# A two-layer SSM and GeGLU kernel: partial sums read in PSUM and added to, block 1's kv by four sums, norms in ScalarE, and additions by transfer

## The chip, the cores and the metric

The kernel runs on one core of a Trainium2 chip. The metric is the time of one execution in microseconds on the device. The profile is one execution seen by the hardware profiler. TensorE (PE in the profile, with its weight loads as PEld), VectorE (DVE), ScalarE (ACT) and GpSimd (POOL) have a program each, run in order, and wait for one another by semaphores; transfers are issued by SyncE's queue (SP) and by POOL.

## What is computed

Two layers, each a long convolution with gating (A) and a gated feed-forward network (B), over 2048 tokens of 576 values:

```python
def _A_ref(q, k, v, shift_k, ssm_k, ssm_D):
    ...
    for t in range(ks):
        k_shift = k_shift + k_pad[:, t:t + S, :] * shift_k[:, ks - 1 - t][None, None, :]
    kv = k_shift * v
    ...
    y_f = kv_f * kf_f[None, :, :, :]
    ...
    y = y + kv * ssm_D[None, None, :]
    return q * y
def _B_ref(x, w_gate, w_up, w_down):
    return (_gelu(x @ w_gate) * (x @ w_up)) @ w_down
x = A_q
x = x + _A_ref(_layernorm(x, axis=-1), A_k, A_v, A_shift_k, A_ssm_k, A_ssm_D)
x = x + _B_ref(_layernorm(x, axis=-1), B_w_gate, B_w_up, B_w_down)
x = x + _A_ref(_layernorm(x, axis=-1), A_k, A_v, A_shift_k, A_ssm_k, A_ssm_D)
x = x + _B_ref(_layernorm(x, axis=-1), B_w_gate, B_w_up, B_w_down)
```

Here kv_f and kf_f are Fourier transforms over time of kv and of ssm_k, padded to twice the length, and y is the transform back, cut to 2048. The convolution's result y does not depend on x, so it is computed once and serves both layers.

## The kernel before

**Feed-forward.** The tokens stand in four chunks of 512. A unit is one layer of one chunk, eight in all, numbered in the order (layer 0, chunk 0), (0, 1), (1, 0), (1, 1), (0, 2), (0, 3), (1, 2), (1, 3). They run in passes [0], [1, 2], [3, 4], [5, 6], [7]; a pass goes three times (a third of the 4608 hidden columns each) over its units. One such visit is twelve tiles of gate/up (L1516: 18 matmuls of 512 columns on half the array's rows each, for gate and up side by side), and for each of four rows of tokens a down projection of 24 matmuls of 288 columns (L1535). ScalarE applies the gelu (L1520), VectorE multiplies (hT, L1521), which frees the tile's PSUM buffer; the pool has three. Unit 0's first visit runs with 256 columns at a time (L1441).

**Between units.** x is gated with y (`gate2_steps`, L1165 and L1172 on VectorE), its mean and variance go through ScalarE (L1137) and POOL (L1129, L1144, L1145), VectorE writes the normalised rows xn (`norm` in `prep`, L1194, and a copy of the first 64 columns behind it, L1196), and `spread` has SP transpose them into xnT by two transfers for each of four rows (L1224). SP's queue also carries the weights, which `weights` holds back while rows are about to come. Unit 0 has its own functions, not touched.

**Convolution.** It is done in four blocks of 512 tokens by short transforms of 512 frequencies, as matmuls of the twiddle matrices W with [128, 288] halves of the data, products in the frequency domain, sums over pairs of blocks, and inverse transforms (`inverse`, L340) into y. Block 0 is done in the startup. For block 1 and for its filter's rest (`h1_rest`, the function's `fwd`), `fwd_eo` makes even and odd sums in the two banks of a PSUM tile with four matmuls (L223), ScalarE copies them to a tile eo (L226), and VectorE's `cross` takes sum and difference (L287). For blocks 2 and 3 and their filters, `quarter` makes four sums of one matmul pair each (L261), ScalarE copies each (L263), and VectorE combines them: `both(0, 2)` and `both(1, 3)` (L238 and L239, sum and difference in place), then `even` (L244) and `odd` (L252). Most of these PSUM tiles come from the pool cps, which has one buffer; eo has four.

**Products and sums.** `prod` multiplies a transformed block K with a transformed filter H, real parts first (part 0: L298 and L302), then imaginary (part 1: two products L301 with H's halves exchanged, and L302). In `step(1)` two blocks are summed for each of four frequency tiles kt: `add` (L550) writes the f32 sum zs, `cross` there calls `Conv.both` (L316) and `shift` calls `shifted` (L321), which joins the result with the block before.

**The order.** A planner writes all engines' programs out while it builds the kernel. It keeps model clocks for TensorE, VectorE and ScalarE (`Pace`, with costs C_... for each operation). After each gate/up tile and each pair of down matmuls `fill` lets queues go on: V and U (convolution work on VectorE; U goes first), vq (gating and norms), aq (ScalarE's sums and squares, one for each call), L and spills (POOL's transfers), and Pq (convolution pieces on TensorE, `run_p`). Pieces of Pq go out in order, in the down projection, and among gate/up tiles where `now` says so: before block 1's y is done (`hurry`, after 60 us of the model or while `fresh` pieces are left), for the last pieces of a quarter (`LATE`), or for a y that vq waits for. In the down projection, `run_p(True)` may take the next piece once per row with a buffer of the pool pr instead of cps. `at_start` says at which visit the sums of a chunk's x (`es`) and its gating and norms (`prep`) are entered.

The lines that the planner uses to let a piece go, and the list of visits:

```python
if max(ready(), 0.0 if other else self.ps_free) > t.pe:
    return False
...
at_start = {(0, 0): [("es", 1), ("prep", 1)], (1, 0): [("x", 2)], (2, 1): [("es", 2)],
            (3, 0): [("prep", 4)], (3, 1): [("x", 3)], (4, 1): [("es", 3)], (4, 2): [("prep", 5)]}
```

Of the kernel before, what the change touches and what calls it, by code (L numbers as in the profile page):

```python
# [36 lines left out]
C_SQ, C_TINY = 0.85, 0.6  # L37
N_KC, N_SM, N_EO, N_HR = 4, 4, 4, 3
C_AC, C_AB = 0.76, 0.76
C_TT, C_ST, C_BN, C_NORM, C_HT, C_GELU, C_EVA, C_EVD = 0.76, 0.82, 0.47, 0.62, 0.69, 0.6, 0.66, 0.76  # L40
# [44 lines left out]
class Conv:  # L85
# [9 lines left out]
    def __init__(self, tc, ctx, pace, A_k, A_v, A_shift_k, A_ssm_k, A_ssm_D, ident, psp, cpsp, ypool):  # L95
        self.tc, self.nc, self.t = tc, tc.nc, pace
        self.k2, self.v2, self.hk = A_k[0], A_v[0], A_ssm_k
# [118 lines left out]

    def fwd_eo(self, src, kt, s, h, scale=1.0):
# [11 lines left out]
    def quarter(self, src, out, h, ready, seen, done):  # L229
# [7 lines left out]
        def both(a, b):  # L237
            tt(out=A[b][:], in0=A[a][:], in1=A[b][:], op=add)  # L238
            nc.vector.scalar_tensor_tensor(out=A[a][:], in0=A[a][:], scalar=2.0, in1=A[b][:], op0=ALU.mult, op1=sub)  # L239
            t.on_dve(2 * C_R4)  # L240
# [16 lines left out]
        def one(i):  # L257
            def run():
                ps = self.ps()
                for s in range(2):  # L260
                    nc.tensor.matmul(ps[:, s, 0:HW], lhsT=self.W[:, 2 * i + s, :], rhs=src()[:, i, cols], start=True, stop=True)  # L261
# [3 lines left out]
                self.ps_free = when  # L265
                if i == 2:
                    self.U.append((when + LAG, 2 * C_R4, lambda: both(0, 2)))
                if i == 3:
                    seen(h)
                    self.U.append((when + LAG, 2 * C_R4, lambda: both(1, 3)))  # L270
# [3 lines left out]
        return [(lambda: max(ready(), self.eo_slot()), 0.25, one(i), ("tail", h, i)) for i in range(RT)]  # L274
# [14 lines left out]
    def prod(self, part, K, H, dst=None, own=False):  # L289
# [9 lines left out]
        else:  # L299
            for s in range(2):  # L300
                nc.vector.tensor_tensor(out=pr[:, s, :], in0=K[:, s, :], in1=H[:, 1 - s, :], op=ALU.mult)  # L301
# [17 lines left out]
    def shifted(self, now, prev, part):  # L319

# [91 lines left out]
    def step(self, m, kv=None, loaded=False):  # L412
# [66 lines left out]
        def fwd(kt, s, h):  # L479
            def run():  # L480
                if s == 0 and h == 0:
                    for k in (kt, kt + 2):
                        kc[k] = self.kcp.tile([P, 2, D], BF16, tag="kc", name="kc")
                eo, slot = self.fwd_eo(self.vt_[m], kt, s, h)
                done = t.on_act(C_EVA, t.pe + 0.49 + LAG)
                self.ps_free = done
# [548 lines left out]
def ssm_geglu_kernel(ctx, tc, A_q, A_k, A_v, A_shift_k, A_ssm_k, A_ssm_D, B_x, B_w_gate, B_w_up,  # L1035
# [151 lines left out]
    def prep(ui, j):  # L1187
# [17 lines left out]
        if j >= lag:  # L1205
            tasks.append(norm(j - lag))
# [419 lines left out]
```

## Time and profile before

| | us |
|---|---|
| median of 3 runs (lowest, highest) | 918.87 (918.66, 918.88) |
| profiled execution: time | 918.66 |
| profiled execution: span, first to last instruction | 916.9 |
| first gate/up matmul of unit 0 | 39.1 |
| gate/up matmuls, L1516, 4968 | 541.7 busy |
| down matmuls, L1535, 2304 | 293.3 busy |
| convolution matmuls among gate/up after 39 us | 13 pieces, the last of the first four directly ahead of the down projection |
| y of block 1, four pieces | 131.7 to 142.2 |
| first matmul of unit 1 | 160.2 |

The span leaves out 1.8 us that the time has around it. The granted TensorE clock was 1.00 throughout. A row of the profile names the line, the engine, the operation, what is written and read, the shapes and the count, then busy time, the mean of one in ns, the engine's idle time just before, and what ended it. In the chain of waits in order of time, the columns are start, length and what, in us. TensorE's matmuls overlap, so two of 288 columns that take 286 ns each in their rows take 0.24 us together in the chain.

### The profile page before, as it was taken

The page shows a single profiled execution, that of the slowest core. Times are in us where ns is not written, and L with a number is a line of the kernel's source. Part 1 is how long each engine was busy: PE and PEld are TensorE (multiplying, and loading weights), DVE is VectorE, ACT ScalarE, POOL GpSimd, SP SyncE. Part 2 cuts the span into 40 slices and gives each one's busy share as a digit, 9 for nine tenths or more (in the row PEclk, how much of TensorE's full clock was granted, in tenths as well). Part 3 has the DMA queues.
Part 4 walks back from the last instruction along what each step waited for, and adds up shares of the span by engine and source line. Part 5 has one row for each costly group of instructions (what it writes and reads, how often), then busy time and mean ns, then how long its engine had stood idle before and what let it go on. Part 6 is the DMA issues. An engine that isn't in the chain of part 4 may idle for free.

```text
span 916.9 us, 19346 instructions
## 1 busy us (share of the span) xinstructions
PE 909.1 (99%) x8214; PEld 528.5 (58%) x8214; DVE 608.1 (66%) x1096; ACT 296.6 (32%) x552; POOL 146.1 (16%) x307
## 2 busy tenths in 40 slices
PE   8999999999999999999999999999999999999998
PEld 6786556465565564655655645646546556556555
DVE  7988977578889889798698898652332335432332
ACT  6863225433314134432224123341121224221211
POOL 3433004201114121130013202220000003000000
PEclk9999999999999999999999999999999999999999
DMA  9998978909518706755733912950720721877620
GB/s 257 329 258 254 176 182 161 261 26 258 157 53 196 238 9 123 191 159 145 180 103 96 250 45 60 170 135 11 146 79 1 156 78 22 164 180 173 140 63 26
DMA packets 128666, 130.85 MB, mean 143 GB/s; under 512 B 43586, under 2 KB 120387, under 8 KB 128580
## 3 DMA queue, kind: packets, MB, share of 16 engines
q1 hardware_dynamic: 119232, 93.47, 47.2%
q0 software_dynamic: 9344, 36.14, 11.7%
q8 instruction: 64, 1.05, 0.5%
q14 instruction: 22, 0.18, 0.1%
q10 hardware_dynamic: 4, 0.01, 0.0%
HBM read 108.35 MB, written 11.80 MB: 131 GB/s over the span
## 4 chain that ended last, share of the span: by engine, by line
PE 98%; DVE 1%; ACT 1%; issue 0%; DVEq 0%; ACTq 0%
PE gu L1516 59%; PE dn L1535 31%; PE gu L1441 3%; PE ps L212 1%; PE cps L340 1%; PE cps L261 1%; PE cps L223 1%; PE ps L340 0%; DVE wx L881 0%; PE cps L212 0%; PE cps L818 0%; DVE wx L884 0%; PE ps L223 0%; ACT junk L1137 0%; PE xps L1334 0%; PE ps L895 0%
## 5 line engine op out<-in xcount | busy, mean ns | idle before, releaser
L1516 PE MATMUL gu<-xnT,wgu 64*128 64x512 bf16 x4968 | 541.7, 376 | 0.0
L1516 PEld LDWEIGHTS <-wgu 64*128 64x128 bf16 x4968 | 239.3, 94 | 294.3 <-issue 7.6
L1520 ACT ACTIVATE ga<-gu 128x512 f32<-128x512 f32 x276 | 164.8, 597 | 504.8 <-PE gu L1516 496.4
L1521 DVE TENSOR_TENSOR hT<-ga,gu 128x512 bf16<-128x512 f32 x276 | 189.2, 686 | 194.8 <-ACT ga L1520 192.9
L1535 PE MATMUL dn<-wd,hT 128*128 128x288 bf16 x2304 | 293.3, 286 | 0.0
L1535 PEld LDWEIGHTS <-hT 128*128 128x128 bf16 x2304 | 223.6, 98 | 65.4 <-issue 9.8
L1571 DVE TENSOR_TENSOR x_c<-x_c,dn 128x576 f32<-128x576 f32 x64 | 48.2, 753 | 60.6 <-PE dn L1535 60.2
L1129 POOL TENSOR_SCALAR nm<-s 128x1 f32<-128x1 f32 x60 | 21.1, 352 | 289.2 <-DVE x_c L1566 186.9
L1137 ACT ACTIVATE junk<-x_c,nm 128x576 bf16<-128x576 f32 x48 | 37.0, 772 | 33.7 <-POOL nm L1129 32.2
L1145 POOL TENSOR_TENSOR rstd<-ve,neghalf_t 128x1 f32<-128x1 f32 x62 | 42.2, 681 | 5.2
L470 POOL DMA_DIRECT2D hr<-Hd x32 | 17.5, 547 | 126.3 <-DVE prod L301 119.9
L263 ACT COPY eo<-cps 128x576 f32<-128x576 f32 x32 | 20.4, 639 | 30.7 <-PE cps L261 30.7
L1441 PE MATMUL gu<-xnT,wgu 64*128 64x256 bf16 x432 | 24.6, 269 | 0.0
L1144 POOL TENSOR_SCALAR ve<-ss 128x1 f32<-128x1 f32 x62 | 17.8, 287 | 38.0 <-ACT junk L1137 37.7
L1557 DVE TENSOR_TENSOR ob<-x_c,dn 128x576 bf16<-128x576 f32 x15 | 11.3, 753 | 18.1 <-PE dn L1535 12.9
L302 DVE TENSOR_TENSOR prod<-prod 128x576 bf16<-128x576 bf16 x48 | 22.0, 458 | 1.6
L1441 PEld LDWEIGHTS <-wgu 64*128 64x128 bf16 x432 | 20.8, 94 | 3.4 <-issue 0.9
L355 POOL DMA_DIRECT2D out_dram<-ob x12 | 6.7, 557 | 86.9 <-DVE ob L1557 80.6
L553 DVE TENSOR_TENSOR zs<-zs,prod 128x576 f32<-128x576 f32 x24 | 18.1, 754 | 0.3
L550 DVE TENSOR_TENSOR zs<-sum,prod 128x576 f32<-128x576 bf16 x24 | 18.1, 754 | 0.3
L187 DVE TENSOR_TENSOR kvt<-k,skc 128x1152 bf16<-128x1152 bf16 x24 | 17.6, 753 | 0.2
L1172 DVE SCALAR_TENSOR_TENSOR x_c<-g_t,rstd,x_c 128x576 f32<-128x576 f32 x16 | 13.1, 818 | 6.8 <-POOL rstd L1145 6.6
(158 smaller groups left out, 560.8 us busy)
## 6 DMA issues: line engine op xcount, KB each, us to landing
wgu<-in_B_w_gate_dram SPq DMA_DIRECT2D x45, 576.0 KB, 5.6
wd<-in_B_w_down_dram SPq DMA_DIRECT2D x30, 864.0 KB, 6.6
wgu<-in_B_w_up_dram SPq DMA_DIRECT2D x45, 512.0 KB, 7.7
hr<-Hd POOLq DMA_DIRECT2D x32, 288.0 KB, 5.1
kr<-Kd POOLq DMA_DIRECT2D x24, 288.0 KB, 4.3
Kd<-kc POOLq DMA_DIRECT2D x12, 288.0 KB, 4.1
k<-in_A_k_dram POOLq DMA_DIRECT2D x3, 1008.0 KB, 7.5
wgu<-in_B_w_up_dram SPq DMA_DIRECT2D x45, 64.0 KB, 7.4
```

Source lines behind the costliest of these rows:

```text
L263: nc.scalar.copy(out=A[i][:], in_=ps[:, :, 0:HW])
L302: nc.vector.tensor_tensor(out=dst, in0=pr[:, 0, :], in1=pr[:, 1, :], op=ALU.subtract if part == 0 else ALU.add)
L550: nc.vector.tensor_tensor(out=f[:], in0=self.halves(pr0[:]), in1=self.halves(pr[:]), op=ALU.add)
L1129: nc.gpsimd.tensor_scalar(out=v["nm"][:], in0=v["s"][:], scalar1=-1.0 / D, scalar2=None, op0=ALU.mult)
L1137: nc.scalar.activation(out=junk[:], in_=get_x(), func=ACT.Square, bias=v["nm"][:, 0:1], accum_out=v["ss"][:])
L1145: nc.gpsimd.tensor_tensor(out=v["rstd"][:], in0=ve[:], in1=neghalf_t[:, 0:1], op=ALU.pow)
L1441: nc.tensor.matmul(pair[:, s, e * 256:(e + 1) * 256], lhsT=w[r0:r0 + HK, k, gi * P:(gi + 1) * P], rhs=xnT[r0:r0 + HK, blk_of[k], tok], sta ...
L1516: nc.tensor.matmul(pair[:, s, :], lhsT=w[r0:r0 + HK, k, gi * P:(gi + 1) * P], rhs=xnT[r0:r0 + HK, b, :], start=(k == 0), stop=(k == NKC - 1))
L1520: nc.scalar.activation(out=ga[:], in_=pair[:, 0, :], func=ACT.Gelu_apprx_tanh)
L1521: nc.vector.tensor_tensor(out=hT[:, fi, :], in0=ga[:], in1=pair[:, 1, :], op=ALU.mult)
L1535: nc.tensor.matmul(part[h][:, h, 0:HW], lhsT=hT[:, fi, at * P:(at + 1) * P], rhs=wd[2 * wb + fi // WT][:, fi % WT, h * HW:(h + 1) * HW], s ...
L1571: nc.vector.tensor_tensor(out=xh, in0=xh, in1=acc[:, :, 0:HW], op=ALU.add)
```

## The change

- `quarter`: the four sums are taken in the order 0, 2, 1, 3; the second of each pair is added in PSUM to the first, after ScalarE has copied the first. So ScalarE's second copy is already the sum, and VectorE only makes the difference as twice the first minus the sum (`apart`). Two pieces share a PSUM tile, are marked "pair" and are not taken by `run_p(True)`; `ps_free` is set 0.25 us later.
- Block 1's kv goes through `quarter` as well, in place of eight `fwd_eo` pieces.
- `h1_rest`: its four `fwd_eo` pieces become an even and an odd piece for each of two s (`fwd_sum`): the even sum over both halves is copied to a spare tile (the tile g_t of the gating), the odd one is added to it in PSUM and copied, and VectorE's `differ` makes the other result from the spare tile and PSUM.
- `prod`, part 1: one product that reads H's halves in reverse order, in place of two.
- Block 1's sums for kt 0 and 2: `begin_sum` has POOL copy the first product into the f32 sum by a transfer, `end_sum` adds the second by an adding transfer. `shifted` for kt 0, part 1 is an adding transfer too. The products are put in a new order, with those of kt 3 and 1 between the sums and `cross`.
- Norms of units 1 to 7 become two activations in ScalarE's queue aq, with a bias that POOL multiplies out; vq holds the gating alone.
- `es` and `prep` of chunk 1 are entered at unit 0's third visit.

```diff
     def shifted(self, now, prev, part, transfer=False):
+        if transfer and part == 1:
+            self.nc.gpsimd.dma_start(out=prev[:], in_=now[:], accum_op=ALU.add)
+            return
...
+    def fwd_sum(self, ps, src, kt, s, e):
+        for i in (e, e + 2):
+            for h in range(2):
+                self.nc.tensor.matmul(ps[:, h, 0:HW], lhsT=self.fwd_w(kt, s, i), rhs=src[:, i, h * HW:(h + 1) * HW],
+                                      start=(i == 0), stop=True, skip_group_check=True)
+    def differ(self, dst, eo, ps):
+        self.nc.vector.scalar_tensor_tensor(out=self.halves(dst), in0=self.halves(eo[:]), scalar=2.0, in1=ps[:, :, 0:HW],
+                                            op0=ALU.mult, op1=ALU.subtract)
...
-        def both(a, b):
-            tt(out=A[b][:], in0=A[a][:], in1=A[b][:], op=add)
+        def apart(a, b):
             nc.vector.scalar_tensor_tensor(out=A[a][:], in0=A[a][:], scalar=2.0, in1=A[b][:], op0=ALU.mult, op1=sub)
-            t.on_dve(2 * C_R4)
+            t.on_dve(C_R4)
...
-        def one(i):
+        def one(n, i):
             def run():
-                ps = self.ps()
+                if n % 2 == 0:
+                    A["ps"] = self.ps()
+                ps = A["ps"]
                 for s in range(2):
-                    nc.tensor.matmul(ps[:, s, 0:HW], lhsT=self.W[:, 2 * i + s, :], rhs=src()[:, i, cols], start=True, stop=True)
+                    nc.tensor.matmul(ps[:, s, 0:HW], lhsT=self.W[:, 2 * i + s, :], rhs=src()[:, i, cols], start=(n % 2 == 0), stop=True,
+                                     skip_group_check=True)
...
-                self.ps_free = when
+                self.ps_free = when + LAG
...
-            for s in range(2):
-                nc.vector.tensor_tensor(out=pr[:, s, :], in0=K[:, s, :], in1=H[:, 1 - s, :], op=ALU.mult)
+            nc.vector.tensor_tensor(out=pr[:], in0=K[:], in1=H[:, ::-1, :], op=ALU.mult)
...
+                nc.gpsimd.dma_start(out=f[:], in_=self.halves(pr[:]))
+                return lambda when: self.pr_free.__setitem__(slot, t.pe + 7.0)
...
+                    nc.gpsimd.dma_start(out=sums[(kt, part)][:], in_=self.halves(pr[:]), accum_op=ALU.add)
+                    at[("zs", kt, part)] = t.pe + 6.0
...
+            for kt, part in ((2, 0), (2, 1), (0, 0), (0, 1)):
+                product(kt, 0, part)
+            for kt, part in both:
+                V(0.0, begin_sum(kt, part), eo_done)
+            for kt, part in both:
+                product(kt, 1, part)
+                V(0.0, end_sum(kt, part))
+            for kt, part in ((3, 0), (3, 1), (1, 0), (1, 1)):
+                product(kt, 0, part)
+            for part in range(2):
+                V(2 * C_AB, cross(0, part), get(("zs", 0, part), ("zs", 2, part)))
+                V(2 * C_TB, shift(0, part))
...
+        if other and len(self.Pq[0]) > 4:
+            return False
...
+            self.rest += [(lambda: own.get("free", 0.0), 0.49, even(s), None, "pair"), (lambda: 0.0, 0.49, odd(s), None, "pair")]
...
+            for lo, hi, c0 in ((0, D, 0), (D, XW, 0)):
+                nc.scalar.activation(out=xn[:, lo:hi], in_=x_c[c][:, j, c0:c0 + hi - lo], func=ACT.Identity,
+                                     scale=v["rstd"][:, 0:1], bias=v["nb"][:, 0:1])
...
-        at_start = {(0, 0): [("es", 1), ("prep", 1)], (1, 0): [("x", 2)], (2, 1): [("es", 2)],
+        at_start = {(0, 2): [("es", 1), ("prep", 1)], (1, 0): [("x", 2)], (2, 1): [("es", 2)],
```

167 lines of the change are left out of this document (83 added, 84 removed).

## Prediction

> **What bounds the kernel now.** I read the page's engine table first, then the chain of waits as a table and in order of time.
>
> ```profile
> PE 909.1 (99%) x8214; PEld 528.5 (58%) x8214; DVE 608.1 (66%) x1096; ACT 296.6 (32%) x552; POOL 146.1 (16%) x307
> PE 98%; DVE 1%; ACT 1%; issue 0%; DVEq 0%; ACTq 0%
> ```
>
> TensorE is busy 99% of the span and 98% of the chain. Its 7.8 us without work lie in the startup and after the last matmul, neither of which this change rebuilds. What must be read is whether its time is work or slow matmuls, and that the chain in order of time shows:
>
> ```profile
> 58.40 0.60 PE cps L223 x4
> 58.99 2.07 PE gu L1441 x36
> ...
> 78.51 0.49 PE cps L223 x4
> 79.00 0.49 PE dn L1535 x4
> ...
> 84.64 23.41 PE gu L1516 x216
> 108.05 11.87 PE dn L1535 x96
> ...
> 131.68 1.09 PE cps L340 x8
> ...
> 223.65 0.24 PE cps L261 x2
> ...
> 236.47 0.35 PE cps L261 x2
> ...
> 553.38 0.49 PE cps L340 x4
> ...
> 565.44 0.60 PE cps L340 x4
> ```
>
> Every undisturbed visit costs 23.41 + 11.87 us, and the pieces join without a hole. So the time is the sum of TensorE's pieces, and a convolution piece has two prices: 0.49 us for four matmuls (0.1225 each) between down-projection matmuls (78.51, 553.38), but 0.60 between gate/up matmuls (58.40, 565.44); likewise 0.24 against 0.35 for two. A piece placed among gate/up costs **0.11 us extra**. Freed VectorE, ScalarE or POOL time brings nothing by itself; only fewer matmuls, fewer pieces among gate/up, or a new wait move the end.
>
> **The change, part by part.**
>
> *Block 1's kv by four sums.* Before, eight pieces of four matmuls at L223 (32); after, eight pieces of two at the new `one` (16), as L261 does for blocks 2 and 3. Each piece falls from 0.49 to 0.24-0.25 (or 0.60 to 0.35): 16 x 0.1225 = **-1.96 us**. Four still fall among gate/up from 58 us on, as before, since the same kv half gates them.
>
> *Partial sums in PSUM.* For blocks 2 and 3 and their filters the matmul count stays at eight per half; the second matmul of a pair adds onto what ScalarE has just copied. It must wait for that copy, but the single cps buffer made it wait before too. The planner now books 0.25 us more per step, so steps lie six down matmuls' time apart instead of five; against that one VectorE addition per pair goes:
>
> ```profile
> L238 DVE TENSOR_TENSOR eo<-eo 128x576 f32<-128x576 f32 x16 | 12.0, 751 | 0.0
> L1194 DVE TENSOR_SCALAR xn<-x_c,nm,rstd 128x576 bf16<-128x576 f32 x28 | 16.1, 575 | 1.1 <-POOL rstd L1145 1.1
> L1196 DVE COPY xn<-xn 128x64 bf16<-128x64 bf16 x28 | 5.3, 191 | 1.0
> L550 DVE TENSOR_TENSOR zs<-sum,prod 128x576 f32<-128x576 bf16 x24 | 18.1, 754 | 0.3
> ```
>
> All 16 at L238 go (-12.0 us of VectorE, off the path). Of the 32 L261 pieces three lie among gate/up (at 199.02, 236.47 and 383.68 in the chain). Bounds: none would (-0.33) or two per group of eight, which the LATE rule allows (+0.55). Slower steps and earlier freed eo slots pull opposite ways; I take 0.
>
> *H1's rest* keeps 16 matmuls as two even and two odd pieces. Each even waits until `differ` has freed the spare tile, and a second odd until VectorE has gone through the quarter's queue (0.77 + 1.64 + 1.54 planned). Added up from the planner's costs, the last odd misses the down projection that ends at 84.6: **+0.11** (bounds 0 and +0.44, all four).
>
> *Reversed read in prod.* Two half products become one of 1152:
>
> ```profile
> 27.26 0.76 DVE L298 TENSOR_TENSOR prod<-kc,h 128x1152 bf16<-128x1152 bf16 x1
> 28.43 0.82 DVE L301 TENSOR_TENSOR prod<-kc,h 128x576 bf16<-128x576 bf16 x2
> ```
>
> The pair takes 0.82, the long one 0.76. Of 40 pairs only the startup's last stands on the path (yb, then x_c at 30.40): **-0.07**. The far bound: if the reversed read runs at one element per cycle, the 1152 cost 0.753 (576 in f32) plus 576 / 0.96 GHz as L550 against L302 suggests, about 1.35 us, +0.53 there.
> The Trainium skill (Vector Engine (DVE) Microarchitecture Reference, section 5.1) asks for an innermost step of +-1 and two-byte operands for the double rate, which this read keeps, but lists an operand with a negative step as not measured. By its condition the term is -0.07, by its caveat +0.53; no row here has such a read.
>
> *Norms to ScalarE*: 28 x (575 + 191 ns) leave VectorE; ScalarE gains two activations each (nearest rows L1137 at 772 and the 128x1 warm-up at 203 ns, so 0.98), POOL one small product (L1129 at 352 ns). ScalarE is 32% busy, so 28 us fit; if they pushed a gelu back, TensorE has three gate/up buffers, some 2 x 1.95 - 0.60 - 0.69 = 2.6 us of slack. The deadline is unit 1:
>
> ```profile
> L1224 SPq DMA_TRANSPOSE xnT<-xn x1: 1264/1264/1264, 155.9 to 155.9; - x1
> DMA to landing us min/median/max: 2.5/2.5/2.5
> ```
>
> Unit 1's last transpose lands at 155.91 + 2.5 = 158.4; its first matmul runs at 160.2. Only 1.7 us spare, and TensorE will come 1.9 earlier. Yet the chain shortens too: row 0's norm no longer stands behind row 2's gate, so the four pairs of transposes (2.5 us each on SP's queue) follow the y pieces' 3.1 us spacing instead of piling up until 157.2. I take 0.
>
> *Adding transfers.* Four VectorE additions (754 ns) become four copying and four adding POOL transfers, two shifts (450 ns) two more. Price unseen; nearest rows for 288 KB:
>
> ```profile
> Kd<-kc POOLq DMA_DIRECT2D x12, 288.0 KB, 4.1
> Hd<-h POOLq DMA_DIRECT2D x4, 288.0 KB, 10.3
> ```
>
> Each sum's second transfer waits on POOL for the first; behind it in POOL stand only later sums, loads and spills. Between sum and `cross` lie four products, about one per gate/up tile, 4 x 1.95 = 7.8 us: at 4.1 hidden, at 10.3 not. I take 4.1 to 4.5 (below): 0. Block 1 ends some 4 us earlier, still inside the third visit's gate/up, so its four L340 pieces keep their 0.11 (bounds -0.44 and 0).
> The Trainium skill (DMA: Bandwidth & Descriptors, section "Anatomy of one DMA") fits 2.0 us plus bytes / 436e3; for 295 KB that is an estimate of 2.7 us, below the 4.1 row, and leaves the sum unchanged.
>
> *VectorE relief later.* Some 30 us less before 570 us (12.0 at L238, 16 norms of units 1 to 4 at 0.77, block 1's 4, 40 x 0.06); block 3's last two y pieces, now among gate/up, should make the down projection: **-0.22** (bound +0.22, all four among gate/up).
>
> Sum: -1.96 + 0.11 - 0.07 - 0.22 = **-2.14 us**, 918.66 to 916.5 for the profiled execution. The median is 0.21 above it, so 916.7.
>
> **Rivals.**
>
> 1. *The gain is eaten by misplaced pieces*: -1.96 + 0.11 + 0.22 + 0.55 = -1.1, time **917.8**. For it: every step is booked later. Against: VectorE is freer at each.
> 2. *Slow reversed read*: 0.53 in the startup, and in block 1 eight products at 0.46 + 1.35 against 1.25 booked, 4.5 us that VectorE (21.0 busy of 23.4 at 84.6 to 108) mostly absorbs, perhaps 0.9 lost: -2.07 + 0.53 + 0.9 = -0.6, **918.2**.
> 3. *The sums land late, and it is slower.* At 10.3 us each, first transfers outlast their four products in the down stretch (4.9) by 5.4 and adding ones theirs by 2.5: `cross` stands 7.9 us at VectorE's head, with hT behind it, and TensorE, whose slack is 2.6, loses 5.3: -2.1 + 5.3, **922.0**. It decides once `cross` is over 4.7 us late. For: the startup's Hd spills needed that long, and in this stretch the DMA engines are just as busy (0.94 at 84.6 to 90). Against: the hr load issued there, at 89.1, landed in 4.5 us.
> 4. *Unit 1 comes late, and it is slower.* The early sums and squares of unit 1 now start only at 119.9, one ScalarE task per tile, to 135.5; then eight squares and norms to about 151, landing near 155.6. If block 1's y came four tiles late (7.8), TensorE at 158.2 would wait 5.2: **922.0**.
>
> **How the numbers follow.** About 0.2% (1.84 us) is what a measurement here can tell from no change. Forecast 0.66 (all faster), rivals 1 and 2 0.10 and 0.04 (both within), 3 and 4 0.11 and 0.09 (slower): faster 0.66, same 0.14, slower 0.20. Without a wait the bounds run from -1.96 - 0.33 - 0.44 - 0.22 - 0.07 = -3.0 to rival 2's; that leaves out 0.20, and I stretch the upper end for a small wait: 915.6 to 919.5.
>
> **What would show it.** Right: 16 matmuls of 288 columns fewer; L223's x4 kv pieces as x2 of 0.24 or 0.35; the rest of the chain still gapless with 23.4 + 11.9 per visit; no L238; products of 1152 at 0.75. Wrong: a TensorE gap at about 95-105 with VectorE behind a DMA (rival 3), or before unit 1's first matmul at 158 (rival 4); more than 13 pieces among gate/up (rival 1).

## The result, and the profile after

The changed kernel takes **928.91 us** (median of 4 runs, 928.52 to 929.27) beside 918.76 (918.63 to 918.88) for the kernel before on the same chip: a ratio of 1.011, 95% interval 1.0093 to 1.0128. It is slower by 10 us, where 2 us less had been forecast. The profiled execution has a span of 926.4 us.

The engine table and the first line of the chain of waits, of the changed kernel:

```profile
PE 910.0 (98%) x8198; PEld 528.9 (57%) x8198; DVE 573.2 (62%) x972; ACT 325.8 (35%) x608; POOL 159.8 (17%) x345
PE 90%; DMA 4%; issue 2%; ACT 1%; DVE 1%; POOL 1%; SPq 0%; POOLq 0%; DVEq 0%; ACTq 0%
```

TensorE has the 16 matmuls less that were forecast (8198 for 8214), and VectorE is 35 us less busy. But TensorE holds 90% of the chain instead of 98%: transfers, VectorE, ScalarE and POOL now stand on the path that sets the end. Who made TensorE wait, in the list of waits by engine (total us, times, longest):

```profile
PE gu L1559 <- DVE hT L1564: 6.4, 1, 6.4
PE gu L1559 <- DMA xnT<-xn: 1.5, 2, 0.8
...
PE gu L1559 <- DVE ob L1600: 0.8, 1, 0.8
```

Before, none of these three was on the list. The first is a hole of 6.4 us in unit 0's second visit, which begins at 82 us. VectorE's timeline there (start, length, line, what; in brackets the idle time before it and its releaser):

```profile
96.34 0.76 DVE L315 TENSOR_TENSOR prod<-kc,hr 128x1152 bf16<-128x1152 bf16 x1 [2.42 <-DMA zs<-prod]
...
98.77 0.68 DVE L1564 TENSOR_TENSOR hT<-ga,gu 128x512 bf16<-128x512 f32 x1
104.40 0.76 DVE L313 TENSOR_TENSOR prod<-kr,H 128x1152 bf16<-128x1152 bf16 x1 [4.95 <-DMA zs<-prod]
...
107.47 0.76 DVE L315 TENSOR_TENSOR prod<-kr,H 128x1152 bf16<-128x1152 bf16 x1 [1.81 <-DMA zs<-prod]
...
108.64 0.68 DVE L1564 TENSOR_TENSOR hT<-ga,gu 128x512 bf16<-128x512 f32 x1
```

The next product cannot be written, because the pool of products has three buffers and an adding transfer (zs<-prod) still reads the one whose turn it is. VectorE runs in order, so hT of the next gate/up tile, planned behind the products, stands too: from 98.77 to 108.64 there is none. TensorE fills the PSUM buffers it has and stops. What the transfers took from issue to landing (the list of DMA issues; KB each, median us):

```profile
zs<-sum POOLq DMA_DIRECT2D x4, 288.0 KB, 5.6
zs<-prod POOLq DMA_DIRECT2D x4, 288.0 KB, 12.7
...
Hd<-H POOLq DMA_DIRECT2D x2, 288.0 KB, 12.8
hr<-Hd POOLq DMA_DIRECT2D x1, 288.0 KB, 13.3
```

The copies are zs<-sum, the adding transfers zs<-prod. The last two rows are plain transfers that POOL issued between and right behind the adding ones, and they took as long: what was slow here was every transfer that POOL issued from 91 us on, and no row shows that adding made it longer. From 95 to 98 us, with three to four of them under way, POOL's queue moved 4 of the 611 packets on the DMA engines; the rest were SyncE's.

The hole costs more than its 6.4 us. The stretches around it, with TensorE's busy time and count, its weight loads, VectorE, ScalarE and POOL, then the granted TensorE clock, the DMA engines' busy share and GB/s:

```profile
104.00:106.00 2.00, 0.00 (x0) 0.00 (x0) 1.22 (x2) 0.00 (x0) 0.00 (x0) 0.81 1.07 229
106.00:108.00 2.00, 0.00 (x0) 0.00 (x0) 0.53 (x1) 0.00 (x0) 0.00 (x0) 0.50 1.26 301
...
110.00:112.00 2.00, 2.00 (x12) 0.81 (x10) 1.67 (x3) 0.01 (x1) 0.00 (x0) 0.50 1.12 213
112.00:114.00 2.00, 2.00 (x22) 1.00 (x20) 1.97 (x5) 0.60 (x1) 0.00 (x0) 0.98 1.15 192
```

While TensorE stands, its granted clock falls to 0.50, and it stays there until 112 us: 12 matmuls in 2 us, then 22. The Trainium skill (TensorE: Matmul & The Clock Gate, Part 1, "The HAM clock gate") says that about 3.4 us of idleness bring the array to half rate and that about as long a busy time brings it back. The trace agrees on the half rate, and roughly on the times: the last matmul ends at 102.97 and the clock falls at 105.25, 2.3 us later; matmuls begin again at 109.37 and the clock is back at 112.07, 2.7 us later. In e14 below the two times are 4.3 and 5.6.

**The account.** I measure a visit's excess as its length over what the undisturbed visits take: 23.42 us of gate/up and 11.87 of down projection, with 0.1225 for each convolution matmul in it and 0.11 for each piece among gate/up. Before, the excess of all visits is 0.82; after, 11.70: 8.09 in that visit, 0.89 + 0.89 at unit 1's start (the second wait above), 0.97 in the visit at 816 us (the third), the rest within 0.05 of before. So 916.9 + 10.88 of excess - 1.96 (16 matmuls) + 0.22 (15 convolution pieces among gate/up instead of 13) + 0.34 (first gate/up at 39.40 instead of 39.06) = 926.4, the span.

The second wait is the one that the deadline of unit 1 had threatened. SyncE's transposes for unit 1:

```profile
L1269 SPq DMA_TRANSPOSE xnT<-xn x8: 1222/1265/1707, 154.6 to 166.0; - x8
```

The last lands at 168.54, 10.1 us later than before (158.43). It costs only 1.8 here, because the hole had already made TensorE late.

### The profile page after: what moved, and what is told of

It is laid out like the page before. It is cut to its first block, busy times and chain, and to the rows that moved or that the text cites. A ratio compares the mean times of both kernels' runs of the same rounds, so it can differ in the third digit from the quotient of the medians.

```text
span 926.4 us, 19300 instructions
## 1 busy us (share of the span) xinstructions
PE 910.0 (98%) x8198; PEld 528.9 (57%) x8198; DVE 573.2 (62%) x972; ACT 325.8 (35%) x608; POOL 159.8 (17%) x345
## 4 chain that ended last, share of the span: by engine, by line
PE 90%; DMA 4%; issue 2%; ACT 1%; DVE 1%; POOL 1%; SPq 0%; POOLq 0%; DVEq 0%; ACTq 0%
PE gu L1559 55%; PE dn L1578 28%; PE gu L1484 3%; PE cps L275 1%; DMA Hd<-H 1%; PE ps L213 1%; DMA out_dram<-ob 1%; PE cps L356 1%; DMA zs<-prod 1%; DMA zs<-sum 1%; ACT junk L1188 1%; PE ps L356 0%; DVE wx L931 0%; PE cps L213 0%; PE cps L868 0%
## 5 line engine op out<-in xcount | busy, mean ns | idle before, releaser
L1196 POOL TENSOR_TENSOR rstd<-ve,neghalf_t 128x1 f32<-128x1 f32 x62 | 39.3, 634 | 5.2
L278 ACT COPY eo<-cps 128x576 f32<-128x576 f32 x40 | 25.5, 636 | 33.5 <-PE cps L275 31.0
L1250 ACT ACTIVATE xn<-x_c,nb,rstd 128x576 bf16<-128x576 f32 (+1 forms) x56 | 33.3, 644 | 9.4 <-POOL nb L1200 9.3
L1195 POOL TENSOR_SCALAR ve<-ss 128x1 f32<-128x1 f32 x62 | 21.1, 340 | 45.3 <-ACT junk L1188 44.7
## 6 DMA issues: line engine op xcount, KB each, us to landing
k<-in_A_k_dram POOLq DMA_DIRECT2D x3, 1008.0 KB, 12.2
```

The source lines that it names most:

```text
L278: nc.scalar.copy(out=A[i][:], in_=ps[:, :, 0:HW])
L1195: nc.gpsimd.tensor_scalar(out=ve[:], in0=v["ss"][:], scalar1=1.0 / D, scalar2=EPS, op0=ALU.mult, op1=ALU.add)
L1196: nc.gpsimd.tensor_tensor(out=v["rstd"][:], in0=ve[:], in1=neghalf_t[:, 0:1], op=ALU.pow)
L1250: nc.scalar.activation(out=xn[:, lo:hi], in_=x_c[c][:, j, c0:c0 + hi - lo], func=ACT.Identity, scale=v["rstd"][:, 0:1], bias=v["nb"][:, 0:1])
```

## The experiments

Letters in the expectations stand for the theories named in them. All times are medians beside the kernel before at 918.7 to 918.8 on the same chip; brackets after a ratio are its 95% interval. The milestones are read from each profile: the last of block 1's shifts, unit 1's rows landed, TensorE's waits and the excess as defined above.

### Transfers away, or less in their way

*e1* sums by `add` and shifts on VectorE again; *e2* keeps the transfers and has four product buffers (the pool xn gives two up for the room); *e3* takes only the sums' transfers back:

```diff
e1, e3
-                V(0.0, begin_sum(kt, part), eo_done)
...
-                V(0.0, end_sum(kt, part))
+                V(C_AC, add(kt, 1, part), eo_done)
e1
-                    self.shifted(nyb[(part, kt, sg)], z[(part, kt, sg)], part, kt == 0)
+                    self.shifted(nyb[(part, kt, sg)], z[(part, kt, sg)], part)
e2
-        self.prp = pool("c_pr", 3)
+        self.prp = pool("c_pr", 4)
-    xnp = pool("xn", 4)
+    xnp = pool("xn", 2)
```

> The changed kernel, with block 1's four sums and both shifts made by VectorE additions again, in the changed order of the products. Theory A (the adding transfers land after 7 to 14 us, a product waits until they have read its buffer, and hT waits behind it): the 6.4 us gap of TensorE in the second visit goes, and with it the slower clock there and the late rows of unit 1, which come later only because block 1 did; 916.3 to 917.3 us, 0.2% under the kernel before. Theory B (the norms in ScalarE make unit 1's rows late by themselves): the gap goes, but TensorE still waits some 1.8 us before unit 1; 918.2 to 919.

> The changed kernel with four product buffers in place of three (and two xn buffers in place of four, to make room); the transfers stay. Theory A (the wait is on the product buffer that an adding transfer still reads): the product that finds its buffer taken comes one product, about 2 us, later, so VectorE's waits on the sums' transfers in front of products (10.1 us in the changed kernel) fall by 2 to 6 us, the gap of 6.4 shrinks by as much, and the time falls to 922 to 927. Rival (the wait is for the finished sums, or the DMA engines' load delays the weights): no change from 928.9 beyond 1 us.

> The changed kernel with the four sums made by VectorE again and only the two shifts as adding transfers. Theory A: the shifts are read first by the y pieces some 15 us after they are issued, and land after 6.6 us, so nothing waits: within 0.3 us of the kernel with no transfers, 916.3 to 917.5. Rival (any adding transfer costs, by the load on the DMA engines or on POOL): 1 us or more above the kernel with no transfers.

e1: 927.09 (926.51 to 927.33), ratio 1.009 [1.0075, 1.0105]. The hole is gone (excess of that visit 0.20), so the product buffers did make it. But the time hardly falls: block 1's last shift comes at 134.3 (before: 129.4), unit 1's rows land at 165.35, and TensorE loses 3.52 + 4.73 us there (beyond what before has in these visits, as in all losses below). e2: 928.67 in one run; the hole's 8.09 falls to 3.46, unit 1's loss rises from 1.8 to 6.6. e3: 928.67 (927.46 to 929.24), ratio 1.0103 [1.0086, 1.012]: 1.6 above e1, and all its runs lie above all of e1's, so the rival of its expectation held. The profiles of the two lie 2.7 apart, 1.6 of it at unit 1 and 1.1 in the visit that begins at 425 us; by which way the shifts' transfers, landed at 118, reach there is not shown. So the hole and unit 1's late rows are two costs that **cover each other**: TensorE arrives late at unit 1 by the one, or waits there for the other. That the transfers are the whole loss is refuted.

### Block 1's kv by four sums, alone on the kernel before

*e4*:

```diff
-            if m > 1:
-                self.Pq.extend(self.quarter(lambda: self.vt_[m], out4, h, get(("kv", h)), seen4, done4))
-                continue
-            for kt in range(2):
-                for s in range(2):
-                    self.Pq.append((lambda g=get(("kv", h)): max(g(), self.eo_slot()), 0.49, fwd(kt, s, h)))
+            self.Pq.extend(self.quarter(lambda: self.vt_[m], out4, h, get(("kv", h)), seen4, done4))
```

> The kernel before with one part of the change alone: block 1's kv through quarter (four sums, both as before), with neither the addition in PSUM nor the transfers nor the norms in ScalarE. The count of TensorE's matmuls falls by 16 of 288 columns at 0.1225 us: 1.96 us less, 916.6 to 917.1, if the pieces stay where they were and VectorE's 2 x 1.5 us more additions hide. Rival (VectorE, fuller in the first visits, finishes block 1 later, and unit 1's rows, 1.7 us early before, come late): 917.5 to 919.

934.09 (932.93 to 935.17), ratio 1.0166 [1.0151, 1.0182]: the part that was to bring the gain loses 15 us by itself. VectorE's timeline there:

```profile
85.39 0.69 DVE L1516 TENSOR_TENSOR hT<-ga,gu 128x512 bf16<-128x512 f32 x1 [1.23 <-ACT ga L1515]
...
90.45 1.56 DVE L252 TENSOR_TENSOR kc<-eo 128x288 bf16<-128x288 f32 x4
...
92.52 1.42 DVE L244 TENSOR_TENSOR kc<-eo 128x576 bf16<-128x576 f32 x2
...
94.46 0.75 DVE L298 TENSOR_TENSOR prod<-kc,hr 128x1152 bf16<-128x1152 bf16 x1
```

No part of kc is ready until all four sums are there: the first product with kc begins at 94.5, and VectorE had nothing else to do at 84 to 85 (idle before the hT at 85.39). The last shift comes at 140.0 instead of 129.4, and TensorE waits 12.2 us in three places for transposed rows (8.2 of them before unit 1, the rest at unit 5, near 609 us). Some 7 us of the excess lie around unit 5, and what makes its rows late was not looked into; so not all of the 15 us is block 1.

### What is left without the transfers: kv as before, norms as before

*e5* is e1 with block 1's kv by `fwd_eo` (the lines of e4's diff put back); *e6* is e1 with the norms on VectorE and the early sums at the first tile:

```diff
e6 (the function prep and the queue's conditions as before the change)
-        at_start = {(0, 2): [("es", 1), ("prep", 1)], (1, 0): [("x", 2)], (2, 1): [("es", 2)],
+        at_start = {(0, 0): [("es", 1), ("prep", 1)], (1, 0): [("x", 2)], (2, 1): [("es", 2)],
```

> As the kernel with no transfers, and block 1's kv by the eight pieces of four matmuls as before, so that of the change the additions in PSUM (blocks 2, 3, filters, H1's rest), the reversed read and the norms in ScalarE are left. New theory C (block 1 is a chain of VectorE work, full from 39 us to its last shift; unit 1's rows follow it by a fixed stretch, and TensorE, 1.7 us late for them before, waits for whatever it is longer): kv's differences are done by 83 to 84 again instead of 86.5, the last shift ends at 128 to 131 instead of 134.3, TensorE waits 0 to 3 us before unit 1 instead of 8.7, and gives back the 1.96 us of matmuls: 918 to 921. Rival (the norms in ScalarE or H1's new pieces make unit 1 late): a wait of 6 us or more stays, 924 or more.

> As the kernel with no transfers, with the norms of units 1 to 7 on VectorE again and chunk 1's sums entered at unit 0's first visit, as before. Theory C: block 1's last shift stays at 133 to 136, and unit 1's rows come within 2 us of 165.4 us; 924 to 929. Rival (norms in ScalarE, one task for each tile, are what makes the rows late): the rows land by 160 and the time falls under 920.

e5: 924.38 (922.69 to 925.67), ratio 1.0061 [1.0046, 1.0076]. Block 1 is now earlier than before (last shift 126.7), and still unit 1's rows land at 163.65. ScalarE's timeline of e5:

```profile
140.82 0.77 ACT L1213 ACTIVATE junk<-x_b,nm 128x576 bf16<-128x576 bf16 x1
...
148.59 0.77 ACT L1213 ACTIVATE junk<-x_c,nm 128x576 bf16<-128x576 f32 x1
...
149.35 4.46 ACT L1275 ACTIVATE xn<-x_c,nb,rstd 128x576 bf16<-128x576 f32 x8
```

The squares of chunk 1's x (x_b) run until 141.5, one for each gate/up tile, because they were entered only at the third visit; the squares of the gated rows (x_c) queue behind them until 149.3, and all four rows' norms behind those. The first row's gating begins at 132.2; the row is written 17 us later, where before the change it took 7.9. As all four rows are written at once, their eight transposes then follow one another on SP's queue, issued from 150.6 to 160.8.

e6: 923.35 (922.77 to 923.69), ratio 1.005 [1.0035, 1.0065]. With norms on VectorE the excess of 1.0 at 816 us is gone, but rows land at 162.64 after a last shift at 133.9: the four sums' share.

### The sums on GpSimd

*e7* adds the partial sums with GpSimd instructions instead of transfers (shifts on VectorE); *e8* besides lets two of ScalarE's tasks go per tile:

```diff
e7
-                nc.gpsimd.dma_start(out=f[:], in_=self.halves(pr[:]))
-                return lambda when: self.pr_free.__setitem__(slot, t.pe + 7.0)
+                return lambda when: None
...
-                    nc.gpsimd.dma_start(out=sums[(kt, part)][:], in_=self.halves(pr[:]), accum_op=ALU.add)
-                    at[("zs", kt, part)] = t.pe + 6.0
+                    nc.gpsimd.tensor_tensor(out=sums[(kt, part)][:], in0=self.halves(pr0[:]), in1=self.halves(pr[:]), op=ALU.add)
+                    at[("zs", kt, part)] = self.pr_free[slot] = max(t.pe, t.dve) + 2.5
e8
         run_aq(min(limit, t.pe + 2.3))
+        run_aq(min(limit, t.pe + 2.3))
```

> The changed kernel with the four sums as GpSimd additions in place of the pairs of transfers, the shifts on VectorE. Theory C: four additions of 0.75 us leave VectorE with no transfer to wait for, so the last shift ends some 3 us before the 134.3 of the kernel with no transfers, and TensorE waits that much less before unit 1: 922 to 925. Rival (GpSimd's additions hold up VectorE or come late themselves): 926 or more.

> As the kernel with the sums on GpSimd, and ScalarE's queue may give out two tasks for each tile instead of one, so that squares and norms of unit 1 need not wait for a tile each. Theory C with the norms as the chain's tail: unit 1's rows come 1 to 3 us earlier again, 919 to 924. If the one task for each tile costs nothing: as the kernel with the sums on GpSimd, within 0.5 us.

e7: 922.31 (921.5 to 925.62), ratio 1.0049 [1.0034, 1.0064]; e8: 921.63 (921.45 to 922.03), ratio 1.0032 [1.0021, 1.0044]. An addition takes 1.27 us on GpSimd and holds no product buffer long: no hole, last shift at 131.8, rows at 160.7, 2.0 us lost at unit 1 (2.3 in e8). Two tasks per tile move no milestone, so that the rate is not what holds ScalarE's queue here.

### One part at a time, on a kernel without the three

*e9* is e5 with e6's edit as well: left are the additions in PSUM for blocks 2 and 3, H1's rest and the reversed read. *e10* is e5 with only the early sums back at the first tile. *e11* is e7 with norms on VectorE, *e12* has besides the shifts of kt 0, part 1 as GpSimd instructions.

> The changed kernel without adding transfers, with block 1's kv by fwd_eo as before, and with the norms on VectorE and unit 1's early sums back at the second visit's first tile: left of the change are the PSUM additions in blocks 2 and 3, H1's rest by two sums, and the reversed read. Theory C (three parts cost: four sums lengthen block 1 on VectorE, norms on ScalarE lengthen the rows' chain to unit 1, transfers block product buffers; nothing else does): no wait before unit 1, last transposes landed by 159, excess over the plain visits under 1.5 us in all, time 918.2 to 919.2. Rival D (H1's rest, whose pieces now stand among block 1's own, or the slower pair steps of the quarters delay unit 1 too): rows land after 161, a wait of 1.5 us or more before unit 1, time 920.5 to 922.5.

> The same as the run before (kv as before, no transfers), but norms in ScalarE as in the change; only unit 1's early sums go back from the second visit's third tile to its first. Theory E (the late entry of unit 1's sums and squares delays its rows): rows land near 159 instead of 163.65, wait before unit 1 under 1 us, some 4 us faster than the run with late entry (924.4), so 920 to 921, with the 1.0 at the visit near 816 and the 1.7 near 425 us still there. Rival F (the norms as ScalarE tasks, one per tile behind the squares, delay them): rows land after 162.5, time 923.5 to 924.8.

> The changed kernel with the four partial sums on GpSimd instead of by transfers, both shifts on VectorE, and the norms on VectorE as before. Theory C: block 1 ends as with GpSimd's sums (last shift near 132), rows land at 159 to 160, wait before unit 1 under 1.5 us, no excess at the visits near 341 and 816 us: 918.0 to 919.6. Rival F' (VectorE then has norms on top of block 1 and rows land at 162 or later): 920.5 to 922.

> The run before with two of block 1's four pairs of shifts on GpSimd as well (1.27 us each there by the sums' row, 0.45 on VectorE). Theory C: VectorE's block 1 ends 0.5 to 1 us earlier, the rows too, 917.2 to 919.2. Rival: the shifts on GpSimd end after VectorE's last, y pieces wait for them, 0 to 1.5 us later than the run before.

e9: **918.26** (918.15 to 919.66), ratio 0.9995 [0.9986, 1.0004], excess 0.62 in all, the last of unit 1's transposes issued at 152.3 (before the change: 155.9). The loss lies wholly in the three parts taken out; H1's rest and the pairs in PSUM cost nothing. e11: 919.27 (918.94 to 919.81), ratio 1.0005 [0.9996, 1.0015]: without transfers and with norms on VectorE, the four sums' 16 matmuls are just eaten (0.88 at unit 1, 0.67 near 341 us, three pieces more among gate/up than in e9). e12: 919.34 (918.76 to 921.33), ratio 1.0007 [0.9997, 1.0016]: no better; the shifts moved are not the last ones.

e10: 928.36, but from 921.03 to 929.21 in five runs, and the profiled one was the shortest. In it the last of unit 1's transposes is issued at 154.1 and there is no wait there: entering the sums early does cure e5's delay. What makes the other runs 7 us longer is none of the expected things. So e10's kernel was run once more for its profile (*e13*), and with it the transfers alone on e9 (*e14*):

> The kernel with kv as before, no transfers, norms in ScalarE and unit 1's sums at the second visit's first tile, once more, for its profile: four of its five times lay at 927.6 to 929.2, and the one profile at 921.0. Theory G (a weight load of gate/up or down that comes late, as wd's did by 1.4 us at 184 in that profile, and a slower clock behind it): in a long run a TensorE gap of 3 us or more stands behind a DMA, and the clock falls after it. Rival H (a gap behind VectorE's or ScalarE's own queue, such as unit 1's or a later unit's rows): the gap stands at a unit's first gate/up matmul, behind transposes.

> The kernel with kv and norms as before (918.3) and the adding transfers put back: four sums and two shifts. Theory A (products wait for buffers that transfers still read): a TensorE gap of 3 to 7 us in the visit from 82 to 108, behind VectorE, and then a slower clock; 922 to 928. Rival I (the stall comes only together with the late kv of the four sums, which make all products fall at once): the excess in that visit stays under 1.5 us, 918.3 to 920.

e13: 927.36. Its list of waits and its down weights:

```profile
PE dn L1603 <- DMA wd<-in_B_w_down_dram: 6.2, 1, 6.2
```

```profile
L1177 SPq DMA_DIRECT2D wd<-in_B_w_down_dram x2: 535/536/537, 173.0 to 192.9; - x2
...
DMA to landing us min/median/max: 19.1/19.1/19.1
```

TensorE stands 6.2 us, from 185.9 in the down projection that begins at 183.8, for weights that SyncE issued at 173.0, and that took 19.1 us beside k's and x_b's loads; with the slow clock behind it the excess is 7.83. Before the change the same load was issued at 162.8. In e10's profile it was issued at 172.7, took 14.5 and the wait was 1.4: the two profiles differ by how late this one transfer lands. Theory G of the expectation holds.

e14: 925.96 (920.57 to 927.44), ratio 1.0069 [1.0044, 1.0094]. Without the four sums, the adding transfers took 6.3, 6.7, 7.2 and 12.1 us, and the hole is there, behind one product that waits for the last of them, issued at 90.3:

```profile
102.42 0.76 DVE L315 TENSOR_TENSOR prod<-kr,H 128x1152 bf16<-128x1152 bf16 x1 [6.15 <-DMA zs<-prod]
103.21 0.46 DVE L316 TENSOR_TENSOR sum<-prod 128x576 bf16<-128x576 bf16 x1
103.58 0.68 DVE L1604 TENSOR_TENSOR hT<-ga,gu 128x512 bf16<-128x512 f32 x1
```

Its excess is 8.83. The transfers cost without the four sums too, and by the product buffers.

### The hold on weights

The planner holds weights back while rows are about to be transposed. The change had replaced "the next task of vq is a norm" by "any norm waits in ScalarE's queue". *e17* is e10's kernel without the second half of that condition; only the order of SyncE's queue differs:

```diff
-            near = xn_made or any(a[3:] for a in aq)
+            near = xn_made
```

> The kernel with kv as before, no transfers, ScalarE norms and early start (921.0 once, 927.4 to 929.2 five times), with one line of the planner changed: weights are held back only while a normalized row waits for its transposes, no longer while norms wait in ScalarE's queue. Only SyncE's queue is in another order. Theory L (wd of the visit from 160 is issued at 173, behind unit 2's first transposes, where before issued it at 162.8, and lands beside k's and x_b's loads): wd is issued before 166, no wait in the down stretch at 183.8, the 1.0 near 810 perhaps still there; 918.4 to 920, all runs within 1. Rival M (the loads of k and x_b make wd late wherever it is issued): the gap at 183.8 stays, median over 925. Rival N (transposes now stand behind weight loads and land late): a wait at a unit's first gate/up matmul, 920 to 924.

**918.38** (918.35 to 918.61), ratio 0.9996 [0.9986, 1.0006]. The load now:

```profile
L1177 SPq DMA_DIRECT2D wd<-in_B_w_down_dram x2: 531/1414/2297, 163.3 to 164.0; - x2
...
DMA to landing us min/median/max: 8.8/8.8/8.8
```

It is issued at 163.3, lands in 8.8 us, and no wait is left; the excess of 1.1 near 810 us is gone as well, where in e10 the transposes from 774 on had put three tiles' weights together behind them at 792 to 799. Norms in ScalarE cost nothing (918.38 beside e9's 918.26). What cost was the late entry of their squares and the longer hold. In the changed kernel itself the load of wd that e13 waits for came even later, at 176.7, but landed in 8.4 us and in time, since TensorE was late as well; of the hold only the wait at 816 us shows there.

### Four sums for half of the columns

*e15* is e9 with block 1's first half of kv columns by four sums and the second as before; *e16* has its partial sums on GpSimd as in e7; *e18* is e16 with norms in ScalarE, entered early, and e17's condition:

```diff
e15
-            if m > 1:
+            if m > 1 or h == 0:
                 self.Pq.extend(self.quarter(lambda: self.vt_[m], out4, h, get(("kv", h)), seen4, done4))
                 continue
```

> The kernel with kv and norms as before and no transfers (918.3), but with block 1's first half of kv columns by four sums and only the second as before: 8 matmuls fewer (-0.98). Theory C (the four sums cost through VectorE's chain at the end of kv, not by their number): the first half is worked while VectorE has room, kc is complete within 1 us of 79.3 and rows land by 160: 917.2 to 918.6. Rival J (each half costs as much): half of the 5.1 us between 918.3 and 923.4, so 920 to 921.5.

> The run before with block 1's four partial sums on GpSimd. Theory C: VectorE has 3 us less in block 1, rows land by 158, no wait before unit 1: 917.1 to 918.2. Rival K (GpSimd's sums come later than VectorE's would and cross waits for them): 918.5 to 920.5.

> The change with what the runs showed to cost taken out: block 1's first half of kv columns by four sums (8 matmuls fewer, -0.98), the second as before; partial sums on GpSimd instead of transfers; shifts on VectorE; norms in ScalarE as in the change, but unit 1's sums from the second visit's first tile and weights not held for norms that wait in ScalarE's queue. Theory C with L (each of the costs was one of these): no wait over 0.5 us in any visit, 917.2 to 917.9, as with norms on VectorE (917.49). Rival N (with the four sums beside them, ScalarE norms land unit 1's rows late after all): a wait of 1 us or more before unit 1, 918.5 to 920.5.

e15: **917.65** (917.42 to 918.15), ratio 0.9988 [0.9979, 0.9998]. e16: **917.49** (917.43 to 917.81), ratio 0.9987 [0.9977, 0.9996]. Both beat both kernels, if by little: kc is complete at 79.1, as in e9, the excess is 0.83, and of the 0.98 us of 8 matmuls less (x8206 below) 0.6 and 0.8 remain beside e9. The first half's sums are worked while VectorE has room; it is the second half's lateness that costs. The engine table of e16, and its sums on GpSimd:

```profile
PE 908.3 (99%) x8206; PEld 528.1 (58%) x8206; DVE 592.2 (65%) x1030; ACT 296.9 (32%) x552; POOL 156.3 (17%) x311
```

```profile
L593 POOL TENSOR_TENSOR zs<-sum,prod 128x576 f32<-128x576 bf16 x4 | 5.5, 1368 | 7.1 <-DVE prod L316 7.1
```

e18: 922.81 (920.77 to 924.55), ratio 1.0049 [1.0035, 1.0063]: worse than e16, though block 1 is as early (last shift 127.9). SyncE's timeline:

```profile
143.33 7.01 SPq L1296 DMA_TRANSPOSE xnT<-xn  x4
150.44 0.63 SPq L1169 DMA_DIRECT2D wgu<-in_B_w_gate_dram  x1
151.11 0.70 SPq L1170 DMA_DIRECT2D wgu<-in_B_w_up_dram  x1
151.85 1.26 SPq L1171 DMA_DIRECT2D wgu<-in_B_w_up_dram  x1
153.21 14.26 SPq L1296 DMA_TRANSPOSE xnT<-xn  x8
```

With weights held only while a row waits, a tile's weights now slip between unit 1's second and third row; the last row lands at 162.33 and TensorE waits 2.6 us. In e17 no weights came between (its eight transposes are one stretch, 143.7 to 156.7). So some longer hold is needed, but not one as long as the change had made it: rival N of that expectation came true by its wait, and the median lies above its range (the profile is that of the shortest run). A rule for it that suits both was not tried.

## Why the prediction was wrong

**Right.** 16 matmuls less, and block 1's kv pieces of two at 0.24 or 0.35; block 3's four y pieces all in the down projection (-0.22); no L238. The reversed read runs like the forward one, so its rival fell:

```profile
L315 DVE TENSOR_TENSOR prod<-kc,hr 128x1152 bf16<-128x1152 bf16 x12 | 9.0, 754 | 2.4 <-DMA zs<-prod 2.4
L313 DVE TENSOR_TENSOR prod<-kc,hr 128x1152 bf16<-128x1152 bf16 x12 | 9.0, 752 | 0.0
```

754 ns beside 752. Where the Trainium skill (Vector Engine (DVE) Microarchitecture Reference, section 5.1) lists a negative step as not measured, these rows show the full rate for a reversed outer dimension.

**Off in size only.** H1's rest has both of a pair's pieces (89.84, 92.49) among gate/up, +0.22 for +0.11; five quarter pieces instead of three (+0.22 for 0, inside the bounds); the startup came 0.34 later for 0.07 earlier, which is within what the start varies by from run to run (39.0 to 39.5 in most profiles here). Together the terms make -1.4 for -2.14. With no new wait the profiled execution would have taken 917.3 by them. The price of a piece among gate/up was itself too low: besides its own 0.11, the gate/up tile next to it takes 2.05 us in the chain of before (132.77, 234.43), where the twelve of an undisturbed visit take 1.95 each. So a piece costs 0.2, and the 0.82 of excess before the change is the nine such pieces behind unit 0's first visit, not waits.

**The step that failed: "Block 1 ends some 4 us earlier".** It counted VectorE's instructions and not when their inputs come. Taking the transfers out shows it (e1): block 1's last two shifts end 4.9 us later than before, not 4 earlier. First the kernel before, then e1:

```profile
128.54 0.82 DVE L321 TENSOR_TENSOR yb<-yb 128x576 bf16<-128x576 bf16 x2
...
133.51 0.82 DVE L337 TENSOR_TENSOR yb<-yb 128x576 bf16<-128x576 bf16 x2
```

In the changed kernel's own trace the next step is the larger one (8.1 of 10.9 us), but with its transfers gone e1 is only 1.8 us faster. The prediction booked the four sums as "16 x 0.1225" on TensorE alone. By e4's rows a half of block 1's kv costs VectorE 1.56 + 1.42 through `odd` and `even` and two differences of 0.76, 4.5 us (with L238's two sums, as in e4 itself, 6.0), against 8 x 0.41 = 3.3 through `fwd_eo`. That is 1.2 us more per half; and `fwd_eo` hands kc over piece by piece, `quarter` only when all sums are there. e4 (a wait of 8.2 us at unit 1 by this part alone), e15 (0.6 below e9 with the first half by four sums) and e6 (5.7 above e15 with the second half so too) settle it. Block 1 is a chain on VectorE, and unit 1 waits at its end, with 1.7 us spare, as the prediction read; its rival 4, priced for rows up to four tiles late, named the right place, and its 0.09 was far too little.

**"At 4.1 hidden ... I take 4.1 to 4.5"** was mis-sized and looked at the wrong waiter. Copies took 5.6 and adding transfers 12.7 us, as long as the plain ones beside them. The Trainium skill (DMA: Bandwidth & Descriptors, "Anatomy of one DMA") gave the estimate of 2.7 for a transfer of that size; the trace differs by a factor of two for the copies and nearly five for the later transfers, and the measurement decides. The DMA engines were full for most of that time (busy share 1.07 to 1.26 in the windows shown, but 0.29 from 103 to 104 us). The prediction let the sums be late only for `cross`; what stood first were the products that needed the transfers' source buffers back, three in number, with hT behind them in VectorE's order. Rival 3 had the place (a hole at 95 to 105, VectorE behind a DMA; 103 to 109 in the trace) and a price near it (5.3 for 8.1), through another wait.

**"Yet the chain shortens too"**, and with it "I take 0" for the norms, failed twice. The new entry at the third visit put chunk 1's early squares, one for each tile, in front of the squares that the norms need (e5, cured in e10). Rival 4 had seen the late entry, with the early squares done by 135.5 and the rows landed near 155.6; in e5 these are 141.6 and 163.65. And `weights`, whose condition the change had rewritten (the line taken out in e17), held SyncE's loads longer, so that wd was issued 10 us later (e13, cured in e17). The prediction counted activations on ScalarE and never followed the hold to SyncE's queue.

**The costs do not add.** Put back alone on e9 (918.26), in medians:

| part put back | us | over e9 | its loss at |
|---|---|---|---|
| block 1's four sums (e6) | 923.35 | +5.1 | unit 1's rows |
| adding transfers (e14; runs from 920.6 to 927.4) | 925.96 | +7.7 | product buffers, 95 to 102 us |
| norms in ScalarE, late entry, hold (e5) | 924.38 | +6.1 | unit 1's rows, 421 and 814 us |
| norms in ScalarE, early entry, hold (e10; runs from 921.0 to 929.2) | 928.36 | +10.1 | wd at 186 us, 809 us |
| norms in ScalarE, early entry, no hold (e17) | 918.38 | +0.1 | none |
| all (the change) | 928.91 | +10.7 | product buffers, unit 1, 816 us |

The first three would be 18.9 together. A TensorE that comes late by one wait has less to wait at the next, which is why taking the transfers away or easing them (e1, e2, e3) moved the time by less than 2 us.

**Left open.** Why transfers on POOL's queue took 12 us and more is not settled: SyncE's packets went first from 95 to 98 us in the changed kernel, but at 103 the engines were mostly idle and the transfers still under way. Nor was it looked into what costs e5 its 1.7 us at 421. Part of e10's spread, whether a run's wd lands after 14.5 us or after 19.1, shows no cause in the order of the program.

## What to carry to other kernels

Before work is moved to a transfer, ask which buffer the transfer keeps and who needs that buffer next: here an addition of 0.75 us on VectorE became a hold of 7 to 13 us on one of three product buffers, in an engine program that runs in order. When fewer matmuls are bought by results that come all at once, price it at the latency of the last consumer: the same edit gained 0.6 us on the half of the work that had slack and lost 5.7 on the half that had none. And when one undone part changes nothing, look whether another wait has taken its place: build up from the version with all suspects out, one part at a time.

## What the runs showed of the hardware

A TensorE wait has a price beyond its length only when it is long. Waits beside the excess of the stretches they fall in: 1.4 us cost 1.5 (e10), 2.6 cost 2.7 (e18), but 4.4 in two places cost 6.7 (e6), 5.5 cost 8.8 (e14), 6.2 cost 7.8 (e13) and 6.4 cost 8.1 (the change). In each of the last four the granted clock stood at 0.50 for 6.8 us (103.1 to 109.9 in e14, 105.3 to 112.1 in the change), and in e10 and e18 it did not fall. What counts is how much of the 6.8 us falls on matmuls: 5.2 us in e6, 5.6 in e14, 3.0 in e13 and 2.7 in the change. Half of that added to the wait gives 7.0, 8.3, 7.7 and 7.8 us, an estimate near the four excesses.

An adding transfer of 288 KB took 6.8 to 14.4 us in the changed kernel. Plain transfers of that size issued on the same queue from 91.8 us on took 12.7 to 13.3 there, and 5.5, 9.9 and 11.2 in e9 (issued at 85 and 86 us), which has no adding transfer; so no run here shows that adding makes a transfer longer. GpSimd's own addition of two 128x576 bf16 tiles into f32 took 1.27 to 1.37. ScalarE's two activations for one normalised row (576 and 64 columns) took 1.19 together (33.3 us for 28 rows), beside 0.77 for the pair on VectorE.
